# Attention in units of all four batch rows, its scores and its outputs two slots apart, with a reordered prologue

## The chip, the core and the metric

The kernel runs on one core of one Trainium2 chip. The metric is device time in microseconds (us) of one execution. The time before is the median of three runs.

## The reference

A decaying linear attention over blocks of 64 positions, followed by a two-layer feed-forward block with a softplus:

```python
# q, k, v: (B=4, H=8, S=768, D=64); lam: (8,); w_in: (512, 2048); w_out: (2048, 512)
for b in range(nb):                       # 12 blocks of 64 positions
    intra = einsum('bhic,bhjc->bhij', qb, kb) * Dmask
    intra = einsum('bhij,bhjd->bhid', intra, vb)
    inter = einsum('bhid,bhde->bhie', qb * lam_pow, kv_state)
    out[:, :, sl] = intra + inter
    kv_state = lam_block * kv_state + einsum('bhsd,bhse->bhde', kb * rev_pow, vb)
x = out, heads side by side               # 3072 tokens x 512
h = x @ w_in
return softplus(h) @ w_out                # 3072 x 512, float32
```

## The kernel before

The 768 positions are cut into six chunks of 128, so a chunk is two blocks for all four batch rows (512 tokens). The feed-forward part runs in slots: slot `s` stands for chunk `s // 16` and one 128-wide slice `f = s % 16` of the hidden layer. `mlp1(s)` makes that slice (12 matmuls of 512 columns: four pairs of heads, three products each, since every operand is a sum of a high and a low part), `chain_act` and `chain_lo` turn it into softplus in a high and a low part, and three slots later (`LAG`) `mlp2(s)` adds its share to the output of the chunk, 12 matmuls again, three for each of the four batch rows. The output of a chunk stays in two PSUM tiles of two banks each (`pair`, tag `o`): one for the batch rows 0 and 1, one for 2 and 3. `evacuate(c)` copies it out: ScalarE takes the even batch rows, VectorE the odd ones, and in the last chunk each of the two takes half of every row.

The attention of the next chunk is computed between these slots. A unit `g` is one chunk, one pair of heads and two batch rows (eight units to a chunk, 48 in all). At every odd slot TensorE has one stage of 64x64 matmuls: `mm_out` of unit `g-1` and `mm_scores_update` of unit `g`, into one PSUM tile of two banks (`work`, tag `t`, a single buffer). VectorE then masks the scores (`mask_scores`), carries the states on (`decayed`: `first_states`, `update_states`) and scales the queries (`q_decay`); ScalarE and VectorE copy the output of `g-1` into the high and low part of `x` (`x_parts`). `mm_out(g)` in the stage two slots later needs all of it. Within a slot every engine takes its work in the order in which the loop writes it: the schedule is the program's order.

All 32 weight blocks of 512 KB come in raw form and are split on the chip into a high and a low part, once, during the prologue and slots 0 to 15: `w_scale` and `w_hi` on ScalarE, `w_bits` (three instructions) and `w_lo` on VectorE, two blocks a slot. `w_lo` of a slot waits for `w_hi` of the same slot, and `w_hi` for `w_bits` of the slot before.

The prologue loads the first chunk in four tiles (`load_first`), warms TensorE with 16 matmuls of zeros, builds the decay tables, and computes the first chunk's attention for all four batch rows at once, one pair of heads after the other, in `begin` (scale keys and queries, scores), `middle` (copy the states on ScalarE, mask on VectorE) and `end` (outputs, `x`). Between these it splits the blocks 0, 1 and 2 and runs parts of `mlp1(0)`. All loads and most stores go through SyncE's queue, in program order, and wait there for a free buffer.

Of the kernel before, what the change touches and what calls it, by code (L numbers as in the profile page):

```python
# [19 lines left out]
NU = 2 * NP  # L20
NG = NCH * NU
# [11 lines left out]
def decay_attention_softplus_ffn(  # L33
    ctx: ExitStack,
    tc: tile.TileContext,
    att0: bass.AP,
    dmaj: bass.AP,
    tmaj: bass.AP,
# [12 lines left out]
    def t8(shape, dt, name):  # L51
        return sb.tile(shape, dt, tag="b8", bufs=20, name=name)
# [4 lines left out]
    def t2(shape, dt, name):  # L57
        return sb.tile(shape, dt, tag="b2", bufs=8, name=name)

    def t1(shape, dt, name):  # L60
        return sb.tile(shape, dt, tag="b1", bufs=4, name=name)

    def th(shape, dt, name):
        return sb.tile(shape, dt, tag="bh", bufs=9, name=name)
# [17 lines left out]
    first, dm, tm, raws = {}, {}, {}, {}  # L82

    def load_first(p):
        first[p] = t8([128, 2, 2, 512], F32, f"first{p}")
        for n in range(2):
            nc.sync.dma_start(out=first[p][:, n], in_=att0[p, :, n])

    n_loaded = NU

    def load_upto(n):
        nonlocal n_loaded
        while n_loaded < min(n, NG):
            g = n_loaded
            for src, to, n_ in ((dmaj, dm, "dm"), (tmaj, tm, "tm")):
                t = t2([128, 512], F32, f"{n_}_{g}")
                nc.sync.dma_start(out=t, in_=src[g // NU - 1, g % NU])
                to[g] = t
            n_loaded += 1

    def q_of(g):
        return dm[g][:, 0:256].rearrange("q (b t i) -> q b t i", b=2, t=2)

    def k_of(g):
        return dm[g][:, 256:512].rearrange("q (b t i) -> q b t i", b=2, t=2)

    def kt_of(g):
        return tm[g][:, 0:256].rearrange("q (b t d) -> q b t d", b=2, t=2)

    def vt_of(g):  # L110
        return tm[g][:, 256:512].rearrange("q (b t d) -> q b t d", b=2, t=2)
# [30 lines left out]
    load_first(0)  # L142
    w_load(1)
    load_first(1)
    load_first(2)
    w_load(2)
    load_first(3)
    w_load(3)
    load_upto(NU + 1)
    w_load(5)  # L150
    load_upto(NU + 2)
# [7 lines left out]
    for _ in range(16):  # L159
        nc.tensor.matmul(warm_ps, lhsT=warm[:, :128], rhs=warm, start=True, stop=True)  # L160
# [65 lines left out]
    def w_hi(ks):  # L226
        nc.scalar.copy(out=w_at(ks)[:, 0], in_=conv[ks[0]].bitcast(F32))  # L227
# [23 lines left out]
    def heads(g):  # L251
        p = (g % NU) // 2
        return slice(2 * p, 2 * p + 2)

    def last_chunk(g):
        return g >= NG - NU

    def k_decay(g, eng):
        kd = t1([128, 2, 2, D], F32, f"kd_{g}")
        if eng is nc.scalar:  # L260
            for t in range(2):
                h = heads(g).start + t
                nc.scalar.activation(kd[:, :, t], kt_of(g)[:, :, t], AF.Copy, scale=rp1[:, h : h + 1])
        else:
            w = rp1[:, heads(g)].rearrange("q (o t w) -> q o t w", o=1, w=1).broadcast_to([128, 2, 2, D])
            eng.tensor_mul(out=kd, in0=kt_of(g), in1=w)
        kds[g] = kd

    def q_decay(g):
        qd = t1([128, 2, 2, T], F32, f"qd_{g}")  # L270
        w = lp[:, heads(g), :].rearrange("q (o t) i -> q o t i", o=1)
        nc.vector.tensor_mul(out=qd, in0=q_of(g), in1=w.broadcast_to([128, 2, 2, T]))  # L272
        qds[g] = qd


    def mm_scores_update(g, w):
        q, k, kd, v = q_of(g), k_of(g), kds.pop(g), vt_of(g)
        for b in range(2):
            for t in range(2):
                cols = slice((2 * b + t) * 64, (2 * b + t + 1) * 64)  # L280
                for s in range(2):
                    r = half(s)
                    nc.tensor.matmul(w[r, s, cols], lhsT=k[r, b, t], rhs=q[r, b, t], start=True, stop=True)  # L283
                    if s == 0 or not last_chunk(g):
                        nc.tensor.matmul(  # L285
                            w[half(1 - s), s, cols], lhsT=kd[r, b, t], rhs=v[r, b, t], start=True, stop=True
                        )

    def mm_out(g, w):
        a, qd, v, st = aa.pop(g), qds.pop(g), vt_of(g), states.pop(g)  # L290
        for b in range(2):
            cols = slice(256 + b * 64, 320 + b * 64)
            for s in range(2):
# [3 lines left out]
            for s in range(2):  # L297
                r = half(s)
                for t in range(2):
                    nc.tensor.matmul(w[half(t), s, cols], lhsT=v[r, b, t], rhs=a[r, b, t], start=False, stop=True)  # L300

    def mask_scores(g, w):
        a = t1([128, 2, 2, T], F32, f"a_{g}")
        for s in range(2):
            r = half(s)
            m = mask[r, heads(g), :].rearrange("q (o t) i -> q o t i", o=1).broadcast_to([64, 2, 2, T])
            nc.vector.tensor_mul(out=a[r], in0=w[r, s, 0:256].rearrange("q (b t i) -> q b t i", b=2, t=2), in1=m)  # L307
        aa[g] = a
# [8 lines left out]

    def update_states(g, w):

        u = [w[half(1 - s), s, 0:256].rearrange("q (b t e) -> q b t e", b=2, t=2) for s in range(2)]  # L320
        st = states[g]
        decayed(g, st[hi], st[lo], lo, u[0])
        if not last_chunk(g):
# [249 lines left out]
```

## Time and profile before

| | |
|---|---|
| median of 3 runs | 636.53 us (636.52 to 636.63) |
| profiled execution, its own time | 638.29 us |
| its span, first to last instruction | 636.5 us |
| TensorE (PE) busy | 601.8 us, 95% |
| VectorE (DVE) busy | 276.5 us, 43% |
| ScalarE (ACT) busy | 202.5 us, 32% |
| moved by DMA | 49.01 MB, mean 77 GB/s |
| mean granted TensorE clock | 0.970 |

The span is cut into 40 slices of 15.9 us in the page's second part; a digit is a busy share in tenths, and PEclk is the granted clock in tenths. The lines "L376" and so on are line numbers of the code above. PEld is the loading of a stationary operand, which overlaps PE.

### The profile page before, as it was taken

To read this page: it belongs to the slowest core of one execution; us is meant where nothing else is said; L and a number is where in the kernel's file an instruction comes from. 1 tells how busy PE (TensorE), PEld (TensorE's weight loads), DVE (VectorE), ACT (ScalarE), POOL (GpSimd) and SP (SyncE) were. 2 spreads that over 40 slices of the span, in tenths; PEclk is the share of its full clock that TensorE was granted. 3 is DMA by queue.
4 is the path that set the end of the run, shared out by engine and by line. 5 is a ranking of instruction groups with operands and counts; after the bars stand their busy time and mean duration, and the time that the engine had idled before them with its cause. 6 is when DMAs were issued, how large, how long until landed. Compare 5 with 4: busy or idle time off the path is not lost.

```text
span 636.5 us, 11987 instructions
## 1 busy us (share of the span) xinstructions
PE 601.8 (95%) x5264; PEld 490.9 (77%) x5264; DVE 276.5 (43%) x548; ACT 202.5 (32%) x337; POOL 7.5 (1%) x16
## 2 busy tenths in 40 slices
PE   5648998889999999999999999999999999999997
PEld 4537877768888888888888888888888888888885
DVE  5259899996433423533433442342342231211111
ACT  3364666662322222312222222222321222322221
POOL 3000000000000000000000000000000000000000
PEclk8577999999999999999999999999999999999999
DMA  8925632241411110411110411111411000100002
GB/s 302 400 93 183 205 144 96 71 166 35 140 44 51 35 50 18 133 51 39 45 50 18 133 35 49 51 35 35 131 36 50 18 2 1 67 0 1 0 1 66
DMA packets 21508, 49.01 MB, mean 77 GB/s; under 512 B 2512, under 2 KB 3536, under 8 KB 21456
## 3 DMA queue, kind: packets, MB, share of 16 engines
q1 hardware_dynamic: 20880, 47.72, 22.4%
q8 instruction: 41, 0.67, 0.4%
q10 hardware_dynamic: 576, 0.52, 0.3%
q14 instruction: 11, 0.09, 0.0%
HBM read 41.95 MB, written 6.29 MB: 76 GB/s over the span
## 4 chain that ended last, share of the span: by engine, by line
PE 81%; DVE 13%; ACT 3%; issue 1%; DMA 1%; SPq 0%; DVEq 0%; ACTq 0%
PE h L363 37%; PE o L376 35%; DVE c L224 3%; DVE c L221 2%; PE w L296 2%; PE w L283 2%; DVE st L313 2%; DVE w L231 2%; DVE c L220 1%; ACT w L227 1%; PE w L300 1%; PE xy L420 1%; DMA first<-in_att 1%; DVE a L307 1%; PE w L285 1%
## 5 line engine op out<-in xcount | busy, mean ns | idle before, releaser
L363 PE MATMUL h<-x,w 128*128 128x512 f32 x1152 | 286.8, 398 | 0.0
L376 PE MATMUL o<-w,g 128*128 128x512 f32 x1152 | 276.3, 389 | 0.0
L363 PEld LDWEIGHTS h<-x,w 128*128 128x128 f32 x1152 | 215.3, 190 | 46.6
L376 PEld LDWEIGHTS o<-w,g 128*128 128x128 f32 x1152 | 216.2, 188 | 44.9
L352 DVE TENSOR_TENSOR g<-l,g 128x512 fp32r<-128x512 f32 x96 | 66.3, 691 | 240.7 <-ACT g L348 240.7
L346 ACT ACTIVATE l<-h 128x512 f32<-128x512 f32 x96 | 57.3, 596 | 274.9 <-PE h L363 216.9
L348 ACT CAST g<-l 128x512 fp32r<-128x512 f32 x96 | 59.6, 621 | 3.1
L331 DVE TENSOR_TENSOR x<-w,x 128x256 fp32r<-128x256 f32 x40 | 16.9, 424 | 72.6 <-ACT x L330 72.6
L313 DVE SCALAR_TENSOR_TENSOR st<-st,lam_c,w 64x128 f32<-64x128 f32 x144 | 44.1, 346 | 1.6
L330 ACT CAST x<-w 128x256 fp32r<-128x256 f32 x40 | 14.9, 372 | 86.0 <-PE w L283 80.8
L296 PEld LDWEIGHTS w<-qd,st 64*64 64x64 f32 x640 | 17.4, 135 | 31.3 <-issue 31.3
L296 PE MATMUL w<-qd,st 64*64 64x64 f32 x640 | 23.5, 232 | 16.9 <-DVE qd L272 16.9
L307 DVE TENSOR_TENSOR a<-w,mask 64x256 f32<-64x256 f32 x80 | 33.4, 417 | 0.5
L227 ACT CAST w<-c 128x1024 fp32r<-128x1024 f32 (+1 forms) x18 | 17.2, 956 | 34.2 <-DVE c L224 34.2
L283 PE MATMUL w<-dm 64*64 64x64 f32 x640 | 26.6, 220 | 1.4 <-DVE x L331 1.4
L285 PE MATMUL w<-tm,kd 64*64 64x64 f32 x576 | 25.8, 221 | 0.0
L283 PEld LDWEIGHTS w<-dm 64*64 64x64 f32 x640 | 23.2, 137 | 1.5 <-DVE x L331 1.5
L285 PEld LDWEIGHTS w<-tm,kd 64*64 64x64 f32 x576 | 22.4, 137 | 0.0
L300 PE MATMUL w<-a,tm 64*64 64x64 f32 x640 | 21.7, 220 | 0.0
L231 DVE TENSOR_TENSOR w<-c,w 128x1024 fp32r<-128x1024 f32 (+1 forms) x18 | 19.8, 1103 | 4.2 <-ACT w L227 3.9
L224 DVE CUSTOM_DVE_ANT_0 c<-raw,c 128x2048 uint16<-128x2048 uint16 (+1 forms) x18 | 20.5, 1138 | 2.4
L221 DVE SCALAR_TENSOR_TENSOR c<-raw,c 128x1024 uint32<-128x1024 uint32 (+1 forms) x18 | 19.9, 1106 | 0.6
(44 smaller groups left out, 216.6 us busy)
## 6 DMA issues: line engine op xcount, KB each, us to landing
raw<-in_wts SPq DMA_DIRECT2D x32, 512.0 KB, 7.2
dm<-in_dmaj SPq DMA_DIRECT2D x40, 256.0 KB, 2.7
tm<-in_tmaj SPq DMA_DIRECT2D x40, 256.0 KB, 2.7
out_dram<-ob SPq DMA_DIRECT2D x20, 256.0 KB, 2.1
first<-in_att SPq DMA_DIRECT2D x8, 512.0 KB, 9.1
out_dram<-ob ACTq DMA_DIRECT2D x4, 128.0 KB, 1.7
out_dram<-ob SPq DMA_DIRECT2D x4, 128.0 KB, 1.7
lam_b<-in_lam SPq DMA_DIRECT2D x1, 4.0 KB, 2.7
```

The costliest lines, as they stand in the source:

```text
L221: nc.vector.scalar_tensor_tensor(out=c, in0=raw_at(ks, 1), scalar=0x80000000, in1=c, op0=ALU.bitwise_and, op1=ALU.bitwise_or)
L224: nc.vector.tensor_add(out=c, in0=c, in1=raw_at(ks, 0))
L283: nc.tensor.matmul(w[r, s, cols], lhsT=k[r, b, t], rhs=q[r, b, t], start=True, stop=True)
L285: nc.tensor.matmul(w[half(1 - s), s, cols], lhsT=kd[r, b, t], rhs=v[r, b, t], start=True, stop=True)
L296: nc.tensor.matmul(w[half(t), s, cols], lhsT=st[r, b, t], rhs=qd[r, b, t], start=True, stop=False)
L307: nc.vector.tensor_mul(out=a[r], in0=w[r, s, 0:256].rearrange("q (b t i) -> q b t i", b=2, t=2), in1=m)
L313: nc.vector.scalar_tensor_tensor(out=to[:, :, t], in0=of[:, :, t], scalar=lam_c[r, h : h + 1], in1=u[:, :, t], op0=ALU.mult, op1=ALU.add,)
L346: nc.scalar.activation(l_tiles[s], h_tiles.pop(s), AF.Softplus)
L348: nc.scalar.copy(out=g_tiles[s][:, 0, :], in_=l_tiles[s])
L352: nc.vector.tensor_sub(out=g[:, 1, :], in0=l_tiles.pop(s), in1=g[:, 0, :])
L363: nc.tensor.matmul(h_tiles[s], lhsT=w[:, i, cs], rhs=x[:, j, :], start=p == 0 and n == 0, stop=p == NP - 1 and n == 2,)
L376: nc.tensor.matmul(o_tiles[c][b // 2][:, b % 2], lhsT=g[:, i, b * 128 : (b + 1) * 128], rhs=w[:, j], start=f == 0 and n == 0, stop=f == NF ...
```

## The change

- Units: a unit is now one chunk, one pair of heads and all four batch rows (`NG = NCH * NP`, 24 units). Its inputs are one tile of 8 KB a partition, loaded in two halves of 512 KB; `load_upto` is called once in four slots, at its end. The four tiles of the first chunk are the first four units.
- Slots: at `s % 4 == 1` a slot has `mm_scores` of a unit with its masking, states and query scaling; at `s % 4 == 3` it has `mm_out` of the same unit and the copies of `x`; at `s % 4 == 0` ScalarE scales the keys of the next unit, in every chunk (before, VectorE did it after the first chunk). Scores and state updates go to the two banks of one `work` tile (scores in bank 0, updates in bank 1), outputs to another one.
- States: the first chunk's states are a copy of the updates (`first_states`), advanced in place by `second_states`.
- Prologue: the same functions as in the loop. The query scaling of the four first units stands first on GpSimd; the order on the other engines is written out by hand; blocks 0 and 1 get their high part on VectorE instead of ScalarE; `w_lo` of block 2 moves into slot 0; there are 30 matmuls of zeros at the start instead of 16, and 18 more in five places between the stages of the first units.
- Output of a chunk: `evacuate` is gone, and `mlp2` copies each batch row out behind its own matmuls, so the copy of row `b` now stands ahead of the matmuls of row `b+1`. In the last chunk ScalarE and VectorE write their halves into two tiles.
- Buffers: tag `b8` 21 for 20, `b2` 4 (now 2 KB for keys, queries and scores), `bl` 1 for the softplus result, `bh` 5 for 9.

```diff
-    def load_upto(n):                       # 256 KB tiles dm and tm, unit by unit
+    def load_upto(n):
+        for g in range(len(units), min(n, NG)):
+            t = t8([128, 2, 2, 512], F32, f"att{g}")
+            for major in range(2):
+                nc.sync.dma_start(out=t[:, major], in_=att[g // NP, g % NP, :, major])
+            units.append(t)
...
-    load_first(0); w_load(1); load_first(1); load_first(2); w_load(2); load_first(3); w_load(3)
-    load_upto(NU + 1); w_load(5); load_upto(NU + 2); w_load(7)
+    load_upto(2); w_load(1); load_upto(4); w_load(5); load_upto(5); w_load(7)
...
+    def mm_scores(g, w):
+        for b in range(B):
...
+                    nc.tensor.matmul(w[r, 0, cols], lhsT=k[r, b, t], rhs=q[r, b, t], start=True, stop=True)
+                    if s == 0 or not last_chunk(g):
+                        nc.tensor.matmul(
+                            w[half(1 - s), 1, cols], lhsT=kd[r, b, t], rhs=v[r, b, t], start=True, stop=True
+                        )
...
     def mask_scores(g, w):
-        for s in range(2): ...              # two multiplications of 64x256
+        nc.vector.tensor_mul(out=a, in0=w[:, 0].rearrange("q (b t i) -> q b t i", b=B, t=2), in1=m)
...
     def mlp2(ss):
-        for b in range(4):
+        for b in range(B):
             for s in ss:
...
+            if not ends:
+                continue
             src = o_tiles[c][b // 2][:, b % 2]
             if c == NCH - 1:
+                nc.scalar.copy(out=parts[0][:, b, 0:256], in_=src[:, 0:256])
+                nc.scalar.dma_start(out=out[rows, 0:256], in_=parts[0][:, b, 0:256])
+                nc.vector.tensor_copy(out=parts[1][:, b, 0:256], in_=src[:, 256:512])
+                nc.sync.dma_start(out=out[rows, 256:512], in_=parts[1][:, b, 0:256])
             else:
                 if b % 2:
+                    nc.vector.tensor_copy(out=parts[0][:, b], in_=src)
                 else:
+                    nc.scalar.copy(out=parts[0][:, b], in_=src)
+                nc.sync.dma_start(out=out[rows, :], in_=parts[0][:, b])
...
+    for p in range(NP):
+        q_decay(p, nc.gpsimd)
+    k_decay(0); begin(0); keep_warm(2); middle(0); k_decay(1); end(0); x_high(0, z[0]); x_low(0, z[0])
+    begin(1); keep_warm(3); middle(1); end(1); x_high(1, z[1]); x_low(1, z[1])
+    k_decay(2); keep_warm(5); begin(2); keep_warm(5); w_scale([0]); middle(2); k_decay(3); w_bits([0])
+    end(2); x_high(2, z[2]); x_low(2, z[2])
+    begin(3); keep_warm(3); middle(3); w_hi([0], nc.vector.tensor_copy); w_lo([0]); w_scale([1])
+    end(3); mlp1(0, range(NP - 1)); x_high(3, z[3]); x_low(3, z[3]); mlp1(0, range(NP - 1, NP))
+    w_bits([1]); w_hi([1], nc.vector.tensor_copy); w_lo([1]); w_scale([2]); k_decay(NP)
     w_bits([2]); w_hi([2])
-    w_lo([2])
...
+        if scores is not None:              # s % 4 == 1
+            w = work(f"w{scores}")
+            mm_scores(scores, w); mask_scores(scores, w)
+            if scores < 2 * NP:
+                second_states(scores - NP)
+            update_states(scores, w); q_decay(scores, nc.vector)
+        if s % 4 == 0 and s and s // 4 + NP < NG:
+            k_decay(s // 4 + NP)
+        if outs is not None:                # s % 4 == 3
+            w = work(f"z{outs}")
+            mm_out(outs, w); x_high(outs, w); x_low(outs, w)
         if 0 < s < last:
             mlp1(s)
         w_load(2 * s + (9 if s < 9 else 7))
+        if s % 4 == 3:
+            load_upto(s // 4 + NP + 2)
```

(In the diff calls that stand on lines of their own are put side by side.)

More of the change, by code (lines that the diff above doesn't have):

```diff
@@ L19 @@
 NP = H // 2
-NU = 2 * NP
-NG = NCH * NU
+NG = NCH * NP
 DM = H * D
@@ L158, in decay_attention_softplus_ffn, with keep_warm @@
     warm_ps = bank("warm_ps")
-    for _ in range(16):
-        nc.tensor.matmul(warm_ps, lhsT=warm[:, :128], rhs=warm, start=True, stop=True)
+    def keep_warm(n):
+        for _ in range(n):
+            nc.tensor.matmul(warm_ps, lhsT=warm[:, :128], rhs=warm, start=True, stop=True)
+    keep_warm(30)
     ramp = spare[:, 3, 0:T]
@@ L368, in mlp2 @@
     def mlp2(ss):
[L369 removed]
+        c = ss[0] // NF
+        ends = ss[-1] % NF == NF - 1
+        if ss[0] % NF == 0:
+            o_tiles[c] = [pair(f"o{c}_{bp}") for bp in range(2)]
+        if ends:
+            parts = [t8([128, B, 512], F32, f"ob{c}_{n}") for n in range(2 if c == NCH - 1 else 1)]
+        for b in range(B):
             for s in ss:
[L371 to L373 removed]
+                f = s % NF
                 g, w = g_tiles[s], w_of(f, 1)
@@ new lines, in decay_attention_softplus_ffn @@
+    k_decay(0)
+    begin(0)
+    keep_warm(2)
+    middle(0)
+    k_decay(1)
+    end(0)
+    x_high(0, z[0])
+    x_low(0, z[0])
+    begin(1)
+    keep_warm(3)
+    middle(1)
+    end(1)
+    x_high(1, z[1])
+    x_low(1, z[1])
+    k_decay(2)
+    keep_warm(5)
+    begin(2)
+    keep_warm(5)
+    w_scale([0])
+    middle(2)
+    k_decay(3)
+    w_bits([0])
+    end(2)
+    x_high(2, z[2])
+    x_low(2, z[2])
+    begin(3)
+    keep_warm(3)
+    middle(3)
+    w_hi([0], nc.vector.tensor_copy)
@@ L477, in decay_attention_softplus_ffn @@
+    w_lo([0])
+    w_scale([1])
+    end(3)
+    mlp1(0, range(NP - 1))
+    x_high(3, z[3])
+    x_low(3, z[3])
     mlp1(0, range(NP - 1, NP))
+    w_bits([1])
+    w_hi([1], nc.vector.tensor_copy)
     w_lo([1])
     w_scale([2])
+    k_decay(NP)
     w_bits([2])
     w_hi([2])
-    w_lo([2])
     def w_group(j):
@@ L493, in decay_attention_softplus_ffn @@
             chain_lo(s - 1)
-        old, new = (w_group(s + 1) if s else []), w_group(s + 2)
-        if old:
+        old, new = (w_group(s + 1) if s else [2]), w_group(s + 2)
+        if s and old:
             w_hi(old)
```

293 lines of the change are left out of this document (97 added, 196 removed).

## The prediction

> **What bounds the kernel now.** I read the page's slices and its chain of work first, then the chain in order of time, then single stretches of the timeline.
>
> ```profile
> PE   5648998889999999999999999999999999999997
> PEclk8577999999999999999999999999999999999999
> PE 81%; DVE 13%; ACT 3%; issue 1%; DMA 1%; SPq 0%; DVEq 0%; ACTq 0%
> ```
>
> TensorE is full from about the tenth slice on, and its clock is low in the first four. The reader should see three regimes. In the last one the chain in order of time holds nothing but matmuls:
>
> ```profile
> 302.51 2.95 PE h L363 x12
> 305.46 2.72 PE o L376 x12
> ...
> 314.71 2.95 PE h L363 x12
> ```
>
> Two slots take 314.71 - 302.51 = 12.20 us, four groups of 12 matmuls take 4 x 2.72 = 10.88 (0.227 a matmul), so one stage of 64x64 matmuls costs 1.32, its switches included. In slots 0 to 15 the chain is VectorE's:
>
> ```profile
> 57.95 0.43 DVE L272 TENSOR_TENSOR qd<-dm,lp 128x256 f32<-128x256 f32 x1
> ...
> 111.56 0.33 DVE x L331
> 115.13 0.60 DVE g L352
> ...
> 129.25 0.60 DVE g L352
> 142.18 0.44 DVE qd L272
> ...
> 142.76 0.34 PE w L296 x8
> ```
>
> Two slots take 129.25 - 115.13 = 14.12 there, 1.9 more than TensorE needs; from the `x` copy to the last `qd`, 111.56 to 115.13, the attention has 3.57 of it and weight splitting and softplus 10.55. The stage of slot 15 starts at 142.76, when VectorE lets it; from there on TensorE sets the time. So the time is: VectorE's end of slot 1 (58.38), its six pairs of slots up to 142.62, then TensorE's remaining work.
>
> **Step 1, the prologue up to VectorE's end of slot 1.**
>
> ```profile
> 1.45 5.49 PE L160 MATMUL warm_ps<-warm 128*128 128x512 f32 x16 [1.45 <-DVE warm L157]
> 8.11 0.91 ACT L410 ACTIVATE own<-first,rp 128x256 f32<-128x256 f32 x2 [6.10 <-DMA first<-in_att]
> 10.16 0.59 ACT L426 COPY us<-xy 128x512 f32<-128x512 f32 x1 [1.15 <-PE xy L420]
> 10.78 0.69 DVE L429 TENSOR_TENSOR own<-xy,mask 128x512 f32<-128x512 f32 x1 [3.98 <-ACT us L426]
> 15.60 0.36 PE L420 MATMUL xy<-first,own 64*64 64x64 f32 x1 [2.40 <-ACT own L410]
> 17.82 0.59 ACT L426 COPY us<-xy 128x512 f32<-128x512 f32 x1 [1.87 <-PE xy L420]
> 30.42 0.69 DVE L224 CUSTOM_DVE_ANT_0 c<-raw,c 128x1024 uint16<-128x1024 uint16 x1
> 31.15 0.62 ACT L227 CAST w<-c 128x512 fp32r<-128x512 f32 x1 [2.54 <-DVE c L224]
> 31.67 0.90 ACT L410 ACTIVATE own<-first,rp 128x256 f32<-128x256 f32 x2
> 35.79 0.27 PE L437 MATMUL z<-own,us 64*64 64x64 f32 x2
> 36.98 0.59 ACT L330 CAST x<-z 128x512 fp32r<-128x512 f32 x1 [1.95 <-PE z L441]
> 8.40:11.85 3.45, 2.04 (x82) 1.66 (x84) 1.07 (x2) 2.30 (x5) 1.19 (x2) 0.98 1.02 417
> 12.00:16.00 4.00, 1.60 (x45) 1.31 (x39) 3.60 (x5) 2.01 (x4) 1.94 (x3) 0.50 1.03 410
> ```
>
> Before, the last pair's keys (31.67) stood behind a weight's `w_hi` on ScalarE (31.15), which waited for `w_bits` on VectorE (30.42 + 0.69); the new order takes this away. From 12 to about 35 us the clock was 0.50: scores to the next copy took 15.60 to 17.82, 2.22 us, where 1.3 is the price at full clock (the stage above), and the outputs of a pair took 35.79 to 36.98, 1.19, once the clock was back. The 16 zero matmuls end their issue at about 6.8, so 14 more at 0.227 hold TensorE to 9.95, and the first scores, done at 10.16 before, are done at 11.25: 1.1 late. The other 18 (0.45 to 1.13 a place) lie in gaps of 1.5 to 1.7 in which TensorE waits for a copy and a mask, or for keys: they cost nothing, and where a gap were gone, a place at most its 1.13.
>
> I take full clock and walk through the new order with these durations (copy 0.6, mask 0.65, keys 0.9, `x` low part 0.6, `w_scale` 1.15, `w_bits` of one block 1.85, a VectorE copy for `w_hi` between 0.43 and 0.69, taken as 0.55, `w_lo` 0.65). Start of the state copies: 11.25, 14.85, 20.1, 23.55. End of the masks: 12.5, 16.1, 21.3, 24.8. Each unit's chain is scores 1.3, copy, mask (which waits for the copy, as at 10.16 and 10.78), outputs 1.2, high and low part of `x`. Block 0 is split at 26.0, the fourth `x` at 27.25, block 1 at 30.3, `w_bits` of block 2 ends at 32.15, its `w_lo` at 33.45. Slot 0's `w_scale` (two blocks, 2.1) runs to 34.8 and `w_bits` (three instructions, 3.2) to 37.1. Slot 1: softplus low part 0.6, `w_hi` to 38.2, `w_lo` 1.1, `w_bits` to 42.5, attention 4.3 (step 2 without `x`): 46.8. Loads: after the first unit (8.1) SyncE's order is unit 1, block 0, units 2 and 3, blocks 1 to 4, unit 4; at 410 GB/s (last row) the 6.8 MB up to unit 4 are there at 24.7, and its keys are wanted at 27.8; block 0 comes at 12 and is wanted at 18.8, block 1 at 18.4 for 24.1. GpSimd's queue has nothing behind the query scaling that stands first on it, and its last pair is needed at 24.8. So VectorE ends slot 1 at 46.8 in place of 58.38: **-11.6**.
>
> **Step 2, VectorE's slots 2 to 13.**
>
> ```profile
> L313 DVE SCALAR_TENSOR_TENSOR st<-st,lam_c,w 64x128 f32<-64x128 f32 x144 | 44.1, 346 | 1.6
> L307 DVE TENSOR_TENSOR a<-w,mask 64x256 f32<-64x256 f32 x80 | 33.4, 417 | 0.5
> L331 DVE TENSOR_TENSOR x<-w,x 128x256 fp32r<-128x256 f32 x40 | 16.9, 424 | 72.6 <-ACT x L330 72.6
> L331 DVE TENSOR_TENSOR x<-z,x 128x512 fp32r<-128x512 f32 x4 | 2.8, 688 | 7.4 <-ACT x L330 7.4
> ```
>
> Twice the width costs 688 - 424 = 264 ns for 256 more columns, 1.03 ns a column, and not twice the time; in the chain neighbours overlap by some 0.09 (424 ns stand there as 0.33). Four slots, one new unit: mask 0.62 (it was four instructions of 0.417), six state instructions of 64x256, so 6 x (0.346 + 128 x 0.00103) = 2.87, two for the queries 0.8, `x` 0.61: 4.90 in place of 2 x 3.57 = 7.14. With 2 x 10.55 for weights and softplus that is 26.0 in four slots; TensorE needs 24.4, so VectorE still leads, and three times this is 78.0 where 142.62 - 58.38 = 84.24 stood. **-6.2**. Bounds: TensorE's 24.4 (-11.0) and twice the old instruction (0, nothing gained). I take the slope since both of its ends are rows. The wait of `w_lo` for `w_hi` that 10.55 contains comes as often as before: the slot behind the masks and the one behind `x` are free of it, the other two pay it. TensorE starts this stretch cold (42.5 to 47 idle) and loses some 3 us there, inside a slack of 3 x 1.55. Slot 3's load and the keys at slot 4 lie behind VectorE.
>
> **Step 3, slots 15 to 95 on TensorE.** As many stages as before with as many matmuls in each; only the one that was half (outputs of the last unit alone) is full: 0.95 / 2, **+0.5**. Keys on ScalarE add 1 us in four slots to an engine that has 24. The single buffers cost nothing while softplus keeps its slot of distance.
>
> **Step 4, the copies inside `mlp2`.** This is the step on which the forecast hangs.
>
> ```profile
> 158.90 2.88 PE L376 MATMUL o<-w,g 128*128 128x512 f32 x12
> 159.73 0.62 ACT L348 CAST g<-l 128x512 fp32r<-128x512 f32 x1
> 160.46 0.59 ACT L395 COPY ob<-o 128x512 f32<-128x512 f32 x1
> 161.08 0.69 DVE L393 COPY ob<-o 128x512 f32<-128x512 f32 x1
> 161.82 0.59 ACT L395 COPY ob<-o 128x512 f32<-128x512 f32 x1 [0.77 <-PE o L376]
> ```
>
> Row 2's matmuls are over at about 161.1 and ScalarE is free at 161.05, yet its copy starts at 161.82, when row 3's matmuls in the other bank of the same tile are over. Row 1's copy on VectorE starts when row 0's on ScalarE ends, and the mask at 10.78 waited for a copy of the other bank. So the program orders all engines on a two-bank tile as a whole. Then row 1's matmuls, now behind row 0's copy, must wait for it: row 0 is done at 159.6, ScalarE is busy to 160.35, the copy ends at 160.97, row 1 starts at 161.02, a stall of 1.44. Row 2 uses the other tile. Row 3 waits for row 2's copy: 0.2 + 0.59 + 0.05 = 0.84. TensorE has nothing else and no slack: 2.28 a chunk, five chunks, **+11.4**. Ends: 0, and 3.1 a chunk with a refill as in 2.95 - 2.72 and 0.2 for each wake-up, 15.5. Behind them no one else waits; stores start no later.
>
> **Step 5, the tail.**
>
> ```profile
> 623.67 8.32 PE L376 MATMUL o<-w,g 128*128 128x512 f32 x36
> 629.31 0.37 ACT L387 COPY ob<-o 128x256 f32<-128x256 f32 x1 [4.19 <-PE o L376]
> 632.03 0.37 ACT L387 COPY ob<-o 128x256 f32<-128x256 f32 x1 [1.48 <-PE o L376]
> 633.30 0.42 DVE L389 COPY ob<-o 128x256 f32<-128x256 f32 x1 [0.44 <-ACT ob L387]
> ```
>
> By the same rule rows 1 and 3 each wait for two copies, 0.2 + 0.38 + 0.44 + 0.05 = 1.07, so +2.14; behind the last matmul stand two copies in place of four, -0.86: **+1.3**. Two output tiles do not part copies that read one PSUM tile. Without the waits it is -0.9.
>
> **Sum.** -11.6 - 6.2 + 0.5 + 11.4 + 1.3 = -4.6. The profiled execution took 638.29 (span 636.5), so 633.7 by its own time; the runs' median is 636.53, 1.76 below it and on the span, so **631.9**.
>
> **Rivals.** *The banks are kept apart singly*: then steps 4 and 5 give -0.9 in place of +12.7, 618.3. For it: the banks differ, and no row before shows a matmul behind a read of the other bank. Against it: three waits in the rows above. [...] No run here shows what the chip allows, only what the program waits for. Chance 0.14.
>
> *The zero matmuls don't hold the clock*: the gaps (up to 0.95 at 15.2 to 16.1, 0.6 before 18.8) leave some stretches 60% filled, and with 2.04 busy of 3.45 us up to 11.85 (quoted above) the clock fell. If it falls at 18.6, two units pay 0.92 for scores and 0.7 for outputs: +3.2, 635.1, hardly told from no change. Chance 0.08. [...]
>
> *The loads of the units stall TensorE*, on the slow side: with 16 weight tiles and four of `x` resident, one tile of 21 is left, so a unit's load starts when the last one's outputs are done, 10.9 us before its scores.
>
> ```profile
> tm<-in_tmaj SPq DMA_DIRECT2D x40, 256.0 KB, 2.7
> first<-in_att SPq DMA_DIRECT2D x8, 512.0 KB, 9.1
> ```
>
> Landing within 9.9 leaves 1.0 for the keys. 2.7 in the quiet stretch speaks for about 5; at 9.1 (all engines loaded) still nothing. From 10.2 on, 16 units of 0.3 eat the gain; at 11 it is +17.6, 649.5. Chance 0.04.
>
> **Chances and range.** The forecast 0.74, by itself 628 to 636 (step 2 and 4's bounds, 2 us in step 1); single banks 0.14 at 617 to 621; cold prologue 0.08; loads 0.04. The range that leaves out at most 2 in 10 and takes in the second case is 617 to 636. 0.2% (1.3 us) is what a measurement here can tell from no change: faster (below 635.3) 0.86, same 0.09, slower 0.05.
>
> **What would show it.** The masks at 12.5, 16.1, 21.3, 24.8 and PEclk near 1.0 through 30 us; slot 1's `qd` ending near 47; 26 us in four slots up to slot 13; four slots at 24.4 later; at each chunk's end two gaps of about 1.4 and 0.8 inside one `mlp2`. No such gaps, and I am 13 too high; a clock of 0.5 before 25 us, 3 too low; keys waiting for a load, far too low.

## The result

| | before | after |
|---|---|---|
| median | 636.58 us (636.52 to 637.09, 4 runs) | 641.23 us (640.66 to 641.91, 4 runs) |
| ratio | | 1.0072, 95% interval 1.0054 to 1.0089 |
| profiled execution, span | 638.29, 636.5 us | 640.66, 638.9 us |
| VectorE ends slot 1 | 58.38 us | 52.05 us |
| last `mlp2` starts | 623.67 us | 624.48 us |
| mean granted TensorE clock | 0.970 | 0.992 |

The changed kernel is slower by 0.7%, where 0.7% faster was forecast. The prediction cut the time at three places, and the profile after is read at the same places. First the page: the slices of TensorE and of its clock, and the chain that ended last.

```profile
PE   8787999998999998999998999999899999899996
PEclk9888999999999999999999999999999999999999
PE 82%; DVE 10%; ACT 5%; issue 2%; DVEq 0%; ACTq 0%
```

The low clock of the first slices is gone and VectorE's share of the chain has fallen from 13% to 10%, as planned. New are 5% of ScalarE where 3% stood, and 2% of "issue": time in which TensorE waited for nothing that the profile shows.

**The prologue.** VectorE's masks of the four first units, and its last instruction in slot 1 (start, duration, engine and line):

```profile
11.87 0.69 DVE L306 TENSOR_TENSOR own<-xy,mask 128x512 f32<-128x512 f32 x1 [4.99 <-ACT st L319]
15.27 0.69 DVE L306 TENSOR_TENSOR own<-xy,mask 128x512 f32<-128x512 f32 x1 [0.25 <-ACT st L319]
23.62 0.69 DVE L306 TENSOR_TENSOR own<-xy,mask 128x512 f32<-128x512 f32 x1 [2.92 <-ACT st L319]
27.02 0.69 DVE L306 TENSOR_TENSOR own<-xy,mask 128x512 f32<-128x512 f32 x1 [0.25 <-ACT st L319]
51.29 0.76 DVE L270 TENSOR_TENSOR qd<-att,lp 128x256 f32<-128x256 f32 x2
```

The masks end at 12.56, 15.96, 24.31 and 27.71, where 12.5, 16.1, 21.3 and 24.8 were forecast: two on time, then 3.0 lost at once and kept. From the last mask to the end of slot 1 (51.29 + 0.76 = 52.05) it takes 24.34 instead of 22.0. Both places have the same mark on TensorE, in the outputs of the second and of the fourth unit:

```profile
16.01 0.34 PE L298 MATMUL z<-own,att 64*64 64x64 f32 x6 [0.27 <-DVE own L306]
18.03 0.21 PE L298 MATMUL z<-own,att 64*64 64x64 f32 x1 [1.68 <-issue]
...
28.18 0.28 PE L294 MATMUL z<-own,st 64*64 64x64 f32 x3
30.42 0.21 PE L294 MATMUL z<-own,st 64*64 64x64 f32 x1 [1.96 <-issue]
```

In the middle of a row of matmuls whose operands are all there, TensorE stops for 1.68 and for 1.96 us. Beside the first stop stand the clock and the DMA share (busy time of PE, PEld, DVE, ACT, POOL in each stretch, then granted clock, DMA share, GB/s):

```profile
12.00:16.00 4.00, 3.44 (x119) 2.69 (x119) 1.94 (x3) 1.81 (x4) 1.79 (x3) 1.00 1.03 410
16.00:20.00 4.00, 2.31 (x46) 1.95 (x47) 0.00 (x0) 0.61 (x2) 1.03 (x2) 0.81 1.02 405
20.00:24.00 4.00, 4.00 (x74) 2.80 (x72) 1.07 (x2) 2.90 (x7) 0.00 (x0) 0.77 1.02 405
```

The DMA engines are full in all three stretches (a share of 1.02 to 1.03), and behind the stop the clock falls to half, from 18.46 on, for 3.41 us. ScalarE's rows show what stop and clock cost together:

```profile
13.71 0.58 ACT L335 CAST x<-z 128x512 fp32r<-128x512 f32 x1 [1.07 <-PE z L298]
19.39 0.59 ACT L335 CAST x<-z 128x512 fp32r<-128x512 f32 x1 [4.16 <-PE z L298]
19.87 0.91 ACT L263 ACTIVATE own<-att,rp 128x256 f32<-128x256 f32 x2
23.00 0.58 ACT L319 COPY st<-xy 128x512 f32<-128x512 f32 x1 [1.10 <-PE xy L282]
```

From the end of its mask to the cast of its `x` the first unit takes 13.71 - 12.56 = 1.15 and the second 19.39 - 15.96 = 3.43. The third unit's scores, from the end of its keys (19.87 + 0.91) to the copy of its states, take 2.22 at half clock, where 1.3 was reckoned. That is 2.28 + 0.92 = 3.2. The next section tells what the stops are.

**Slots 2 to 15.** The chain in order of time, at its ends:

```profile
104.04 0.42 DVE qd L270
...
117.04 1.13 ACT raw L205
118.17 0.80 ACT kd L263 x2
...
119.01 0.27 PE w L282
```

VectorE's eight slots 2 to 9 take 104.46 - 52.05 = 52.41, so 26.2 in four, where 26.0 was forecast. Then the chain leaves VectorE: the keys of the eighth unit (`kd`) stand behind `w_scale` (`raw`) on ScalarE, and TensorE's scores wait for them:

```profile
118.61 0.27 PE L282 MATMUL w<-att,kd 64*64 64x64 f32 x1 [0.87 <-ACT kd L263]
129.61 0.76 DVE L270 TENSOR_TENSOR qd<-att,lp 128x256 f32<-128x256 f32 x2
131.16 0.28 PE z L294 x8
```

VectorE ends slot 13 at 130.37, so its twelve slots took 78.32 (78.0 was forecast). The stage of slot 15 starts at 131.16, 0.79 later, where 0.14 stood before (142.62 to 142.76). So it comes 79.11 behind slot 1 where 84.38 stood: -5.3 instead of -6.2.

**The slots behind it** go as forecast: two pieces of the chain four slots apart start at 307.86 and 332.26, 24.40 us. And at a chunk's end, here the first one's, all engines in order of time:

```profile
147.23 0.84 PE L385 MATMUL o<-w,g 128*128 128x512 f32 x3
...
148.59 0.58 ACT L402 COPY ob<-o 128x512 f32<-128x512 f32 x1
...
149.22 1.65 PE L385 MATMUL o<-w,g 128*128 128x512 f32 x6 [1.14 <-ACT ob L402]
150.29 0.69 DVE L400 COPY ob<-o 128x512 f32<-128x512 f32 x1 [0.88 <-PE o L385]
150.91 0.58 ACT L402 COPY ob<-o 128x512 f32<-128x512 f32 x1 [1.74 <-PE o L385]
...
151.55 0.96 PE L385 MATMUL o<-w,g 128*128 128x512 f32 x3 [0.68 <-ACT ob L402]
...
152.35 0.85 PE L368 MATMUL h<-x,w 128*128 128x512 f32 x3
```

Three matmuls, a wait for ScalarE's copy, six, a wait, three. From the first matmul to the next group 152.35 - 147.23 = 5.12 instead of 2.72: 2.4 us, 2.28 by the forecast. The view of waits sums the ten waits at the five chunk ends, and two more of the tail (us in total, times, longest):

```profile
PE o L385 <- ACT ob L402: 9.1, 10, 1.1
PE o L385 <- DVE ob L396: 1.8, 2, 0.9
```

**The tail**, from the last `mlp2`:

```profile
624.48 4.24 PE L385 MATMUL o<-w,g 128*128 128x512 f32 x18
...
628.76 0.37 ACT L394 COPY ob<-o 128x256 f32<-128x256 f32 x1 [2.83 <-PE o L385]
...
629.16 0.42 DVE L396 COPY ob<-o 128x256 f32<-128x256 f32 x1 [2.51 <-ACT ob L394]
...
629.64 3.01 PE L385 MATMUL o<-w,g 128*128 128x512 f32 x12 [0.92 <-DVE ob L396]
...
633.58 1.65 PE L385 MATMUL o<-w,g 128*128 128x512 f32 x6 [0.92 <-DVE ob L396]
635.27 0.37 ACT L394 COPY ob<-o 128x256 f32<-128x256 f32 x1 [2.20 <-PE o L385]
```

638.9 - 624.48 = 14.42 where 636.5 - 623.67 = 12.83 stood: +1.6.

### The profile page after: what moved, and what is told of

Same layout as the page of the kernel before. It is cut to its first block, busy times and chain, and to the rows that moved or that the text cites. A ratio compares the mean times of both kernels' runs of the same rounds, so it can differ in the third digit from the quotient of the medians.

```text
span 638.9 us, 11805 instructions
## 1 busy us (share of the span) xinstructions
PE 609.5 (95%) x5296; PEld 491.4 (77%) x5296; DVE 231.2 (36%) x360; ACT 209.6 (33%) x335; POOL 7.0 (1%) x16
## 4 chain that ended last, share of the span: by engine, by line
PE 82%; DVE 10%; ACT 5%; issue 2%; DVEq 0%; ACTq 0%
PE h L368 37%; PE o L385 36%; DVE c L213 3%; PE w L280 2%; DVE c L210 2%; PE warm_ps L147 2%; PE z L294 2%; PE z L298 2%; DVE st L311 1%; DVE c L209 1%; DVE w L220 1%; ACT ob L402 1%; DVE g L357 1%; ACT c L203 1%; ACT l L351 1%
## 5 line engine op out<-in xcount | busy, mean ns | idle before, releaser
L342 DVE TENSOR_TENSOR x<-z,x 128x512 fp32r<-128x512 f32 x24 | 16.6, 690 | 48.5 <-ACT x L335 48.5
L311 DVE SCALAR_TENSOR_TENSOR st<-st,lam_c,w 64x256 f32<-64x256 f32 x72 | 31.7, 480 | 0.9
L280 PEld LDWEIGHTS w<-att 64*64 64x64 f32 x640 | 21.2, 135 | 7.3 <-issue 5.6
L294 PEld LDWEIGHTS z<-qd,st 64*64 64x64 f32 x640 | 17.5, 136 | 11.6 <-issue 11.5
L282 PE MATMUL w<-att,kd 64*64 64x64 f32 x576 | 23.8, 222 | 2.6 <-ACT kd L263 2.4
L294 PE MATMUL z<-qd,st 64*64 64x64 f32 x640 | 21.5, 226 | 4.4 <-DVE qd L270 4.4
L280 PE MATMUL w<-att 64*64 64x64 f32 x640 | 24.7, 222 | 0.0
L282 PEld LDWEIGHTS w<-att,kd 64*64 64x64 f32 x576 | 20.6, 135 | 3.4 <-ACT kd L263 3.4
L263 ACT ACTIVATE kd<-att,rp 128x256 f32<-128x256 f32 x40 | 18.1, 501 | 12.5 <-DMA att<-in_att 12.5
L298 PE MATMUL z<-a,att 64*64 64x64 f32 x640 | 20.5, 221 | 0.0
```

Of the source, the lines that this page charges most:

```text
L280: nc.tensor.matmul(w[r, 0, cols], lhsT=k[r, b, t], rhs=q[r, b, t], start=True, stop=True)
L282: nc.tensor.matmul(w[half(1 - s), 1, cols], lhsT=kd[r, b, t], rhs=v[r, b, t], start=True, stop=True)
L294: nc.tensor.matmul(w[half(t), s, cols], lhsT=st[r, b, t], rhs=qd[r, b, t], start=True, stop=False)
L311: nc.vector.scalar_tensor_tensor(out=to[:, :, t], in0=of[:, :, t], scalar=lam_c[r, h : h + 1], in1=u[:, :, t], op0=ALU.mult, op1=ALU.add,)
```

## The experiments

Theory A says that the copies inside `mlp2` cost some 14 us because the program orders a two-bank tile as a whole. Theory E says that the rest of the miss lies in the prologue, where TensorE runs out of instructions: an instruction block is fetched by the same DMA engines as the loads and comes late behind them. Rivals were a clock that the zero matmuls do or don't hold, and loads that are late by themselves. The runs are told in this order; every kernel was timed beside the kernel before (medians 636.4 to 637.0), and the ratios are to that.

**Copies behind all four rows.** In the changed kernel the loop over copies is taken out of the loop over matmuls:

```diff
-            if not ends:
-                continue
+        for b in range(B if ends else 0):
             src = o_tiles[c][b // 2][:, b % 2]
```

> The changed kernel with the copies of a chunk's output written behind the matmuls of all four batch rows, as before the change; the rest as changed. Theory A (TensorE stands still inside mlp2 because a two-bank PSUM tile is ordered as a whole): in the changed kernel the last mlp2 of a chunk takes 5.10 us where 2.72 are its matmuls, so 5 x 2.38 = 11.9 go, and of the tail's 1.6 as well: 641.2 - 13.5 = 627.7, with no gap inside those groups. Rival B (the copies are then late for the next chunk's first matmuls, so the wait only moves): between 636 and 641, with a gap in front of the next mlp2. Rival C (the long mlp2 is TensorE waiting for weights or softplus, not for copies): unchanged, 641.

628.38 us, ratio 0.987 (0.9849 to 0.9891): 12.9 less than the changed kernel. No wait of TensorE for a copy of `ob` is left in its view of waits.

**One-bank tiles.** The copies stay where the change put them, but each pair becomes two tiles of one bank (`o` and the prologue's `xy`):

```diff
-        return ps.tile([128, 2, 512], F32, tag="o", bufs=2, name=name)
+        return [ps.tile([128, 512], F32, tag="o", bufs=4, name=f"{name}_{n}") for n in range(2)]
...
-                        o_tiles[c][b // 2][:, b % 2], lhsT=...
+                        o_tiles[c][b // 2][b % 2], lhsT=...
```

> The changed kernel, copies inside mlp2 as changed, but the four output banks and the prologue's score banks are eight tiles of one bank each in place of four pairs. Theory A: row b+1's matmuls no longer wait for row b's copy; only the order of the program's tiles made them wait, not the chip: 11.9 at the chunk ends and 2.1 in the last group go, and in the prologue each mask starts with the copy of the states and not 0.6 behind it (up to 2.4): 625 to 627. Rival D (the chip itself keeps TensorE from writing one bank while another engine reads the next): the groups stay at 5.1 us and the time at 639 to 641, or the matmuls of those groups get slower without a visible wait.

626.16 us, ratio 0.9842 (0.9827 to 0.9857). The memory is the same and the order of the instructions is the same; only what the program takes to be one thing differs. What was expected in the prologue doesn't show: slot 1 ends at 53.51, with both stops of TensorE in place. The last `mlp2` runs through:

```profile
613.43 8.32 PE L385 MATMUL o<-w,g 128*128 128x512 f32 x36
```

and its tail is 625.7 - 613.43 = 12.27. TensorE writes in one go until 621.75 (613.43 + 8.32). In the 622.35 us version below, which has the same tiles, it writes until 617.09 (608.77 + 8.32) while ScalarE and VectorE copy other banks from 613.05 on. The 2.2 us between this run and the one before aren't explained in full; some 0.5 lie in the tail (12.8 with the copies behind).

**The kernel before with copies inside.**

```diff
     def mlp2(ss):
         for b in range(4):
             ...matmuls of row b...
+            if not ends:
+                continue
+            ...copies and stores of row b, from evacuate...
-            evacuate((s - LAG) // NF)
```

> The kernel before with one edit: the copies of a chunk's output stand behind each batch row's matmuls inside mlp2, as the change has it. Theory A: 5 x 2.3 to 2.4 at the chunk ends and 1.3 to 1.6 in the tail: 636.6 + 13.3 = 649.9. Rivals B to D and any theory that puts the loss on the units or the loads: 636 to 638.

650.29 us, ratio 1.0216 (1.0199 to 1.0233), +13.9. The same waits as after, in a kernel with nothing else changed:

```profile
PE o L379 <- ACT ob L396: 9.1, 10, 1.1
PE o L379 <- DVE ob L390: 1.8, 2, 0.9
```

So theory A is shown from both sides: added to the kernel before, the copies cost what taking them out of the changed kernel brings.

**Loads of unit 4 and of blocks 3 to 6 held.** They are issued behind the third unit's `x`, by a one-column memset of the tile on VectorE that the load must wait for:

```diff
-    w_load(5)
-    load_upto(5)
-    w_load(7)
+    w_load(3)
...
     x_low(2, z[2])
+    held = t8([128, 2, 2, 512], F32, "att4")
+    nc.vector.memset(held[:, 0, 0, 0:1], 0.0)
+    ...the two loads of unit 4...
+    w_load(7)
```

> The changed kernel with the loads of the fifth unit and of the weight blocks 3 to 6 held back until VectorE has the third unit's x (about 24 to 27 us), so that the DMA engines are idle from about 20 us to there. Theory E (in the prologue TensorE ran out of instructions twice, 16.35 to 18.03 and 28.45 to 30.42, because its instruction blocks of 16 KB queue behind the loads): the second gap goes (2.0 us), the first one stays since the units' own loads still run; the fetches come without the even distance of 6.2 us that they have in the changed kernel; VectorE ends slot 1 at about 50 in place of 52.05, if the blocks 3 and 4 arrive by 34: 639 to 640. Rival F (the gaps are waits for another engine, hidden from the trace): both gaps stay, 641 or, with late weights, more.

639.11 us, ratio 1.004 (1.0025 to 1.0055); the interval just touches that of the changed kernel. The second stop is gone, the first stands (17.50 to 19.18). Slot 1 ends at 51.42, where about 50 was expected. What TensorE waits for is in the trace's DMA records. The page of the changed kernel has a queue for instructions (packets, MB, share of 16 engines):

```profile
q8 instruction: 41, 0.67, 0.4%
```

That is 41 packets of 16 KB. Their first ones, and TensorE's stops without a wait, for the runs that bear on it (us; "after matmul" counts TensorE's matmuls from its first):

```
                    blocks arrive (first to last byte)         TensorE stops after matmul
after               15.49-16.60  21.70-22.81  27.91-29.00      221: 16.35-18.03  475: 28.45-30.42
loads held          16.58-17.66  20.29-21.22  26.28-27.51      221: 17.50-19.18
no zero matmuls     16.41-17.49  22.85-23.92  29.13-30.20      221: 17.14-18.91  475: 31.05-31.73
1 bank              17.05-18.15  23.14-24.18  29.13-30.16      221: 16.74-19.52  475: 29.55-31.54
1 bank, held        15.88-16.98  19.32-20.40  24.94-25.83      221: 15.79-18.27
1 bank, all held    11.46-12.42  19.88-20.91  24.54-25.49      none
2 banks, all held   14.03-14.96  22.60-23.53  27.63-28.83      none
two buffers         13.03-14.02  20.56-21.54  24.52-25.85      348: 22.06-22.89
unit 2 at once      14.05-17.41  21.65-22.65  25.31-26.48      221: 16.41-18.66
```

TensorE goes on 1.25 to 1.53 us after a block has landed, and these stops come after the matmuls 221, 348 and 475, 127 apart, whatever stands there. In none of the 14 traces, the two of the kernel before among them, does it pass one of these three places less than 1.25 us after the landing. With its weight load each, 127 matmuls are 254 instructions; with those of TensorE's sequencer there are 512 from the first stop of the changed kernel to its second, 256 to each 127 matmuls. That one packet of 16 KB stands for these 256 is inferred from the stops, which end behind the landings. In the changed kernel the first three blocks come 6.21 us apart, at a DMA share of 1.01 to 1.04; with loads held the second comes 3.7 us behind the first (3.4 with one-bank tiles). The traces don't show when a block is asked for. That it waits behind the loads is inferred from what holding them changes.

Three gaps over 0.5 us called "issue" are left out of the table (0.74 us twice without the zero matmuls, 0.66 with two buffers). They stand in front of the first matmul of a unit's outputs, where in other units TensorE waits for the copy of the states.

**No zero matmuls between the stages.** The 18 are left out, the 30 at the start stay:

```diff
-    keep_warm(2)
...
-    keep_warm(3)
...
```

> The changed kernel without the 18 zero matmuls between the stages of the prologue. Theory K, they keep the granted clock: without them more of the windows between 11.7 and 52 us of the trace stand at half clock (the changed kernel had three such, each 3.4 us, against two of 23.9 and 13.7 us in the kernel before), TensorE's matmuls there take twice their time, VectorE's end of slot 1 comes 2 to 4 us later, and the time is 643 to 645 us. Theory N, the clock falls by the gaps in the supply of instructions and not by what the zero matmuls fill, and TensorE isn't what ends the stages: 640.5 to 642 us, the same as the changed kernel. Fewer instructions also bring the gaps at the block borders later by 18 matmuls.

641.84 us, ratio 1.007 (1.0051 to 1.0089): the same as after. The clock did fall, for 17 us from 19.87 on:

```profile
20.00:24.00 4.00, 2.44 (x66) 2.20 (x66) 1.04 (x2) 3.24 (x8) 0.00 (x0) 0.50 1.03 407
28.00:32.00 4.00, 2.40 (x48) 2.16 (x48) 1.72 (x3) 1.72 (x3) 0.00 (x0) 0.50 1.03 408
```

So half of theory K holds, and its price doesn't. Counted from the first mask slot 1 ends 40.7 us later, where the changed kernel has 40.2: TensorE at half clock, with 18 matmuls less to do, finishes nearly within the waits that are there anyway. The expectation that 18 fewer matmuls move the borders was wrong in kind: the first stop comes after the 221st matmul again, with other work around it, so the border goes by the count of TensorE's matmuls.

**One-bank tiles and held loads together.** The edit is the sum of those two.

> The changed kernel with one-bank tiles and with the loads of unit 4 and of the weight blocks 3 to 6 held behind the third unit's x. If the two causes add (the copies at the chunk ends by the two-bank tiles, 15 us; the gap in the instructions of the third unit's outputs, 2 us), this is 2 us under the kernel with one-bank tiles alone: 624 us. If what the held loads brought is hidden behind another wait of the prologue, 626 us.

624.69 us, ratio 0.9797 (0.9774 to 0.9819): the two add, 1.5 us below one-bank tiles alone where 2 were expected. The second stop is gone here too.

**Early loads held too.** GpSimd's query scaling of units 2 and 3 moves behind the held loads with them, which the diff leaves out.

```diff
-    load_upto(2); w_load(1); load_upto(4); w_load(3)
+    load_upto(2)
...
     middle(0)
+    hold(2); w_load(1); load_upto(4); w_load(3)    # hold: memset, then the two loads
```

> As the run before, with units 2 and 3 and the weight blocks 0 to 2 held behind the first mask as well. If the first gap (1.7 us inside the second unit's outputs) is an instruction block that queues behind the loads, the block lands before TensorE needs it, the gap is gone and the time is 1.5 to 2 us under the run before: 622 us. Rival: the unit loads now come too late for the gates of slots 2 and 3 or for the second pair of k decays, and the time is the same or up to 4 us longer: 624 to 628 us.

622.35 us, ratio 0.9768 (0.9743 to 0.9794); the interval overlaps that of the run before. The first block now lands at 12.42 and no stop for instructions is left. Of the rival a part is there as well: TensorE's third scores wait for keys whose load came late, and slot 1 ends 3.3 us before the changed kernel's.

```profile
19.11 0.27 PE L284 MATMUL xy<-att,own 64*64 64x64 f32 x1 [1.44 <-ACT own L265]
48.03 0.76 DVE L272 TENSOR_TENSOR qd<-att,lp 128x256 f32<-128x256 f32 x2
```

**The kernel before once more**, unchanged, for its profile.

> The kernel before, unchanged, with another profile. If the profiled execution that the prediction was made from was a slow one of its kind (own time 638.29 against a median of 636.5), this profile has a span of 634.5 to 635 us, and VectorE's end of slot 1 or the granted clock of the prologue differs by the 1.8 us. If the profile itself costs that time, its span is again 636.5 us.

636.69 us, ratio 0.9992 (0.9979 to 1.0004), span 634.8: the first of the two is met. Slot 1 ends 1.5 us before the 58.38 of the prediction's profile, and the rest is equal (577.9 and 578.1):

```profile
56.46 0.42 DVE L272 TENSOR_TENSOR qd<-dm,lp 128x256 f32<-128x256 f32 x1
```

The two executions differ in when the clock stepped. In the profile of the prediction it rose to 1.0 at 4.88, fell at 11.71 and stayed at 0.5 for 23.9 us; in this one it rose at 7.29, fell at 14.12 and was up again from 20.94 to 27.77. From its first rise to 60 us it stood at half for 37.5 us there and for 27.3 here. Over the executions of this kernel whose mean clock is known, clock and time go together: 639.1 us at 0.962, 638.2 to 638.4 at 0.970, 637.6 at 0.973, 635.9 to 637.1 at 0.975 to 0.984.

**All loads held, two-bank tiles.** The changed kernel with the held loads of the 622.35 us version.

> The changed kernel with its two-bank tiles, and with units 2, 3 and 4 and the weight blocks held as in the last but one run. If the 5.3 us that step 1 of the prediction fell short by are the two stops of TensorE for instructions and what follows from them, VectorE's end of slot 1 comes 3.5 to 4.5 us before the changed kernel's 52.05, and the time is 637 us (636 to 638), the stops at the chunk ends left as they are. Rival: the two causes are not independent, the loads held brought time with one-bank tiles alone (626.2 to 622.4) and bring 2 us at the most here, as the loads of unit 4 alone did: 639 us.

639.64 us, ratio 1.0044 (1.0028 to 1.0059). My expectation failed, and the rival's number is met. No stop for instructions is left, but in the profiled execution TensorE waits 0.95 and 1.39 us for the keys of units 2 and 3, the clock is at half speed in three stretches (3.4, 3.4 and 6.8 us) before 58.2 us, and slot 1 ends at 53.01. The price of the stops can't be read from this run, since late loads took their place. One difference to one-bank tiles can be seen: here the third mask (23.42) waits for the copy of its unit's states (22.82), which stands on ScalarE behind a weight block whose load came late. With one-bank tiles the mask doesn't wait for that copy; in the next run it starts at 19.55 and the copy at 20.86.

**Two buffers for the softplus result** in the 622.35 us version (`bufs=1` to `bufs=2` for tag `bl`).

> The fastest version so far (one-bank tiles, loads held, 622.35 us) with two buffers instead of one for the softplus result, which ScalarE waits for in four places of the changed kernel (8.1 us together). Theory: that wait ends no stage, since VectorE is busy through them: 622.4 us, the same within 1 us. Rival: ScalarE's wait delays the gates behind it and with them mlp2 in slots 2 to 14: 1 to 3 us less, 620 to 621 us.

622.84 us, ratio 0.9783 (0.9756 to 0.981): the same, as step 3 had it. Its profile is worth more for the prologue, because nothing stopped TensorE between its second and third mask:

```profile
14.49 0.68 DVE L308 TENSOR_TENSOR own<-xy,mask 128x512 f32<-128x512 f32 x1
19.55 0.69 DVE L308 TENSOR_TENSOR own<-xy,mask 128x512 f32<-128x512 f32 x1 [1.80 <-PE xy L284]
```

5.06 us, where the prediction had 5.2 and the changed kernel 8.35. (It has one-bank tiles, with which the mask doesn't wait for the copy.)

**Whole rows in the last stores** of the same version.

```diff
-            if c == NCH - 1:
+            if c == NCH:
```

> The same version with whole rows in the last chunk's copies and stores, as in the kernel before, instead of halves. Read from the trace, from the start of the last mlp2 to the end of the span: 12.23 us with halves, 12.83 us in the kernel before. If the halves are what makes the difference, 12.8 us here; if the one-bank tiles do, 12.2 us. The whole time 622 to 624 us.

622.6 us in one run. The expectation sets the two kernels wrongly against each other, since the kernel before has halves too; only the comparison with the halves of the same version counts. From the last `mlp2` (608.77) to the end of the span (620.9) it is 12.13 with whole rows and 12.23 with halves: the halves are worth nothing here. VectorE's half starts when ScalarE's half ends, as in the rows of the tail above (629.16 against 628.76 + 0.37, with the wait put down to ScalarE's `ob`): the program lets the two copies of one bank follow one another. What the chip would allow was not tried.

**Unit 2 loaded at once.** In the 622.35 us version only unit 3 and the weight blocks stay behind the first mask.

```diff
-    load_upto(2)
+    load_upto(3)
...
-    hold(2); w_load(1); load_upto(4); w_load(3)
+    hold(3); w_load(1); w_load(3)
```

> The fastest version (one-bank tiles, loads held; 622.35 us) with unit 2 loaded at once again; unit 3 and the weight blocks stay behind the first mask. In the trace of that version no stop for instructions is left, but the k decays of units 2 and 3 wait for their loads and TensorE for them, 1.44 and 0.99 us. Theory: with one unit less in the queue at 11.8 us the first instruction block still lands near 11.5 us, both waits for keys go, and the time is 620 us (619.5 to 621). Rival: unit 2's load is still under way when the first instruction block is fetched, TensorE stops after its 221st matmul again, and the time is 622 to 624 us.

623.4 us, ratio 0.9772 (0.9745 to 0.9799): not told from 622.35. The 620 us expected did not come; in the trace the rival is what happened. In this execution the first mask came 1 us later, and the first block came from 14.05 to 17.41, after the memset at 12.80 had let the held loads go. The stop is back:

```profile
18.66 0.21 PE L300 MATMUL z<-own,att 64*64 64x64 f32 x1 [2.25 <-issue]
```

**All runs in two terms.** The end of slot 1 (end of `qd` on VectorE) and the rest of the span:

| kernel | first mask starts | slot 1 ends | rest | span |
|---|---|---|---|---|
| before, prediction's profile | 10.78 | 58.38 | 578.1 | 636.5 |
| before, once more | 10.74 | 56.88 | 577.9 | 634.8 |
| before, copies inside | 10.80 | 59.35 | 591.5 | 650.9 |
| after | 11.87 | 52.05 | 586.9 | 638.9 |
| after, loads held | 13.02 | 51.42 | 586.4 | 637.8 |
| after, no zero matmuls | 12.54 | 53.26 | 586.7 | 640.0 |
| after, all loads held | 12.88 | 53.01 | 586.4 | 639.4 |
| after, copies behind | 12.62 | 53.05 | 573.2 | 626.2 |
| one-bank tiles | 12.48 | 53.51 | 572.2 | 625.7 |
| and loads held | 11.53 | 50.54 | 572.2 | 622.7 |
| and all loads held | 11.10 | 48.79 | 572.2 | 621.0 |
| and two softplus buffers | 11.31 | 48.86 | 572.1 | 621.0 |
| and whole last stores | 11.49 | 48.84 | 572.1 | 620.9 |
| and unit 2 at once | 12.15 | 50.39 | 572.2 | 622.6 |

The rest takes four values and no others: 578 with 48 small units, 591.5 with these and the copies inside, 586 to 587 with the change, 572 to 573 with the change and no matmul behind a copy of another bank. Whatever is done in the prologue moves the first term alone. The prologue's 11 to 13 us to the first mask vary from run to run: after and "copies behind" have the same instructions there and 11.87 and 12.62, the clock having risen at 4.81 and at 6.36 us while the 30 zero matmuls ran.

Counted from the first mask, which takes most of this chance out, slot 1 ends 40.2 us later in the changed kernel, 38.4 with loads held and 40.1 with all loads held. With one-bank tiles it is 41.0, 39.0 with loads held, and 37.7, 37.6 and 37.4 in the three versions with all loads held. The forecast was 35.0 (46.8 against 11.85).

## Why the prediction was wrong

By its own terms, in the profiled executions: forecast 633.7, measured 640.66, 7.0 more. (By the medians it is 631.9 against 641.23, 9.3 more: 1.8 of the other 2.3 are the step from the sum to the time, told below, and 0.6 are that the profiled execution was the shortest of its four.)

- **Step 1, the prologue: -11.6 forecast, -6.3 measured. This is the step that failed, and 5.3 of the 7.0.** The walk through the order was right in its links (masks on time twice; 5.06 us from the second to the third mask in a run with one-bank tiles where nothing stopped TensorE) and had no term for the supply of instructions: it assumed that TensorE has each instruction as soon as its operands are there. The first stop with the clock that fell behind it cost 3.15 between the second and the third mask (3.2 by ScalarE's rows above). In all seven profiles with a stop at this place the clock fell 0.4 to 1.8 us behind its end; in the four changed kernels without one it stayed at 1.0 until 27 us or later. The second stop cost most of the 2.34 behind the fourth mask: with that stop alone taken away, in the run with held loads, the stretch took 22.62, so 1.7 of them. Between 0.4 and 1.0 is left over in all seven versions without it (22.38 to 22.97 against 22.0), and where that lies was not taken apart. Holding the loads does not give the whole 5.3 back: with one-bank tiles it brought 3.3 to 3.7 us, counted from the first mask, and with two-bank tiles next to nothing, since keys and weights then came late. So the two stops are shown as the missing term; of its price the 1.7 are shown by taking the stop away, and the 3.15 are read from one trace. Why the profile before did not show it: its first three blocks landed at 16.54, 24.16 and 30.96 as well, but TensorE, at half clock and waiting for keys, came to the three places only at 20.14, 27.30 and 38.45. The change took these delays away and ran into the landings.
- **Step 2: -6.2 forecast, -5.3 measured.** The price of 78.0 for twelve slots was right within 0.4 (78.32). I put the keys in slots divisible by four at nothing, hidden behind VectorE; in slot 12 they stand behind `w_scale`, TensorE waits 0.87 for them, and the stage of slot 15 starts 0.79 behind VectorE instead of 0.14. That is the other 0.6, shown by the rows of after and not tried apart.
- **Steps 3 and 4: +11.9 forecast, +12.4 measured** from the stage of slot 15 to the last `mlp2`. The rows of the profile before that showed an idle engine not taking a finished row carried this step, and the experiments bear it out in both directions, +13.9 with step 4 and its tail alone on the kernel before, -12.9 and -15.1 without it on the changed one. The rival of banks kept apart is false for the program as written. The chip had no need of the wait: with one-bank tiles it is 626.2, which is 7.9 above the rival's 618.3, about as much as the forecast itself was short.
- **Step 5: +1.3 forecast, +1.6 measured.** Each wait is 0.92 as the profile counts it (1.07 by the forecast), and the 12 matmuls behind a wait take 3.01 where 12 in the stream take 2.88.
- **The step from the sum to the time.** I took 1.76 off because the profiled execution was that much above the median, as if that went with the kernel. It went with one execution's clock, as the kernel before showed once more: its extra time lay in slot 1's end, behind a longer stretch at half clock, in a prologue that the change rebuilds. Without the deduction the forecast is 633.7; and with slot 1 of the second profile (56.88) step 1 would have been -10.1.
- **The zero matmuls.** The rival of the cold prologue (+3.2) has the clock partly right: it fell at 18.46, close to its 18.6 (my estimate, for which I gave no row), but behind the stop and for 3.41 us, and cost 0.92 at the third unit's scores. What the 18 matmuls themselves are worth is small: 641.84 without them against 641.23. All steps of the clock seen in the traces are whole multiples of 3.413 us apart (in the changed kernel's from 4.81 to 18.46 four, from there to 21.88 one). What makes the clock step was not shown.
- **Loads that stall TensorE** cost nothing in the changed kernel: behind the first unit ScalarE waits for a unit's load in eight places, 2.4 us at the most, and TensorE waits for keys behind none of them. They came in only where I held them myself. This was the only way to a slower kernel that the chances had (0.04 of their 0.05), so slower came for a reason that stood in no rival.

Open is when a block is asked for. The first one can come ahead of the held loads or behind them (from 11.46 and from 14.05 on), and of the versions at 622 to 623 us some have a stop left and some have none.

## What to carry to other kernels

When a copy is moved up between matmuls, give it a tile of its own bank: a tile of several banks is one thing for the program's order, and at a chunk's end here that turned 10 us of gain (626.16 us) into 5 of loss. When a prologue is packed tighter, count TensorE's instructions as a load too: look for "issue" in front of matmuls whose operands are ready, and let the loads that are not needed yet start later. Before a forecast is scaled from one profiled execution to a median, ask in which stretch that execution lost its time, and whether the change keeps that stretch.

## What was not expected of the hardware

- Instruction blocks of 16 KB are counted by the page (41 packets, 0.67 MB, 0.4%) among the packets of the 16 DMA engines that carry the data. With these at a share of 1.01 to 1.04 the changed kernel's first three blocks landed 6.21 us apart, and TensorE stopped for 1.68 and 1.96 us (0.7 to 2.8 in the other runs) at a border, 127 matmuls with their weight loads or a multiple of that after the last. The first matmul behind a stop comes 1.25 to 1.53 us after the landing, and none came sooner in any trace. In one run a single block took 3.4 us (14.05 to 17.41).
- The steps of the granted clock lie whole multiples of 3.413 us apart in the traces, and their phase against the program differs from run to run: the first rise was at 4.4 to 7.5 us. With the same instructions the first mask started at 11.87 with a rise at 4.81 and at 12.62 with one at 6.36; with one-bank tiles, in two runs whose loads differ, at 11.10 with one at 4.44 and at 12.48 with one at 7.49.
- Half the clock for 17 us of the prologue, with the 18 zero matmuls left out, gave 641.84 us against 641.23, which isn't told from nothing.
- Splitting a row between ScalarE and VectorE gained nothing (12.23 against 12.13), since by the program's order the two halves of one bank are copied one after the other (629.16 after 628.76 + 0.37).
